# One issue table in place of a hand-written order: a chunked recurrence followed by a GELU block on one core

## The chip, the cores and the metric

The kernel runs on one core of one Trainium2 chip. The core has five engines that run in parallel, each through its own queue in program order: TensorE (PE) multiplies matrices and, as a separate instruction, loads their stationary operand (PEld); VectorE (DVE), ScalarE (ACT) and GpSimd (POOL) do elementwise work; SyncE (SP) issues transfers. Transfers are also issued here from the queues of ACT and POOL. The metric is the device time of one execution in microseconds (us); lower is better.

## The reference

Two blocks follow each other. The first is a recurrence over 768 time steps, for 4 batches and 8 heads, with a 40 x 40 state per head:

```python
for t in range(S):                                   # S = 768
    y[:, :, t] = einsum('bhd,bhde->bhe', r_t, state)
    Sa = einsum('bhde,bhe->bhd', state, a_t)
    state = state * w_t[:, :, None, :] - einsum('bhd,bhe->bhde', Sa, b_t)
    state = state + einsum('bhd,bhe->bhde', v_t, k_t)
```

The second takes the output as x with 3072 rows of 320 and computes `gelu(x @ w_in) @ w_out` with the exact GELU and an inner width of 2048. All inputs of the recurrence are 32-bit floats; the two weight matrices come as 64-bit floats, so the kernel reads 10.5 MB of weights (2 x 320 x 2048 x 8 bytes) and turns them into 32-bit floats itself.

## The kernel before

The 768 steps are cut into 12 chunks of 64 steps (`C = 64`, `NCH = 12`). Inside a chunk the recurrence is written as matrix products. For chunk c these are the steps, by the names of their functions and the tiles that the profile shows:

- `logs`, `sums`: ACT takes the logarithm of the decay w, PE sums it over time (`wT_ps`, `cum`), ACT takes exponentials (`wpT`, `en`, `part`).
- `turn_a`, `turn_b`, `turn_k`, `turn_v`, `turn_r`, `scale_a`, `scale_b`, `scale_k`: the inputs are transposed and scaled by the decay. For the first chunks PE does the transposes (`aT_ps`, `nT_ps`, ...), and ACT copies them out; for later chunks DVE does it with a stream transpose from tiles that are loaded in pairs.
- `make_N`, `make_A`, `make_RV`: products of 64 x 64 blocks, masked by DVE (`N`, `A`, `VR`).
- A triangular matrix has to be inverted for each chunk. N is written to device memory by SP (four transfers, L615), read back as 128 rows (`Nb`, two transfers, L664), and POOL runs 31 column steps of a multiply and an add each (`start_inverse`, L672 and L674) on `W`. The result goes back over memory (`store_inverse`, L686; `fetch_inverse`, L696 and L700), and `corner` and `joined` (`J`) complete it. Chunk 0 uses five rounds of PE products instead (`squares`, tile `sq`), each with an ACT copy, a DVE transpose and a DVE add between one round and the next.
- `make_av`, `make_X`, `make_sa`, `make_saT`, `make_M`, `make_y2`, `make_QY`: the chain through the state, ending in the two tiles `QY`.
- `outputs`: DVE makes `xt`, the new state `st`, and SP moves a few rows of `xt` between partitions with 11 transfers (L894, L897). `turn_state` transposes the state.

The MLP of a chunk (`mlp`) has four rounds of `ph` products with w_in (L993, 20 per half of the round's output, a GELU each on ACT), and then `po` products with w_out: 32 plain ones for the first three chunks (L1010), seven products of half blocks after that (`seven`, L946). It is a generator; `fill()` lets it issue its next piece between two recurrence steps.

The weights are converted by `to_float`: per piece, DVE and ACT steps (L319, L320, L321, L324), then either two more DVE steps (L327, L328) or two ACT steps and two POOL steps (L330 to L333). There are 10 pieces of w_in and 16 of w_out. w_in must be converted before the first `ph` of a column range, w_out before the first `po`.

The order is written out by hand, and no scheduler changes it: a long list of calls for chunks 0 to 2 with conversions between them (L1059 to L1242), then a loop over the chunks from 2 on (L1244), which issues loads two chunks ahead. Each call issues all instructions of its step, on all engines, at once. All PSUM tiles come from one pool of four equal buffers in rotation (`duo`, L96); a call of `keep(n)` lets the next `duo` run n x 128 columns of a product of no use first, so that PE stays occupied.

```python
    def duo(name):
        pt = psum.tile([P, 2, 512], FP32, tag="duo", name=name)
        while asked:
            n = asked.pop()
            mm(pt[:, 0, :n * P], ident, cum_m.unsqueeze(1).to_broadcast([P, n, P]))
        return pt
```

Of the kernel before, what the change touches and what calls it, by code (L numbers as in the profile page):

```python
# [19 lines left out]
def kernel(  # L20
# [12 lines left out]

# [23 lines left out]
    asked = []  # L90

    def keep(columns):

        asked[:] = [columns]

    def duo(name):  # L96
        pt = psum.tile([P, 2, 512], FP32, tag="duo", name=name)
        while asked:
            n = asked.pop()
            mm(pt[:, 0, :n * P], ident, cum_m.unsqueeze(1).to_broadcast([P, n, P]))  # L100
        return pt

# [8 lines left out]


    def ring(name, n, shape, zero, eng):
        tiles = []
        for i in range(n):
            t = const.tile(shape, FP32, name=f"{name}{i}")
            if zero is not None:
                eng.memset(zero(t), 0.0)
            tiles.append(t)
        turn = [0]  # L120

        def take():
            turn[0] += 1
            return tiles[(turn[0] - 1) % n]
        return take
# [4 lines left out]
    def whole(t):  # L130
        return t


    def unused(t, eng):
        for x in range(2):
            eng.memset(t[x * HP + BL:(x + 1) * HP, :, BW - BL:D + BL], 0.0)


    NT = 3

    NB = 4
    NS = 3
    paired = {n: const.tile([P, G * H, BW], FP32, name=n + "_pairs") for n in ("a", "v", "r")}
    w_tile = const.tile([P, G * DM + REST], FP32, name="w_tile")


    extra = const.tile([P, 4 * G * H * HP], FP32, name="extra")
    b_rows, k_rows = ([const.tile([P, G * DM + REST], FP32, name=f"{n}_rows{i}") for i in range(2)] for n in "bk")
# [3 lines left out]

    raws = {}

    def rows_of(src, c, e):

        return src[G * e:G * (e + 1), :, c * C:(c + 1) * C, :].rearrange("g h t d -> t (g h) d")

    def fetch(c, n, src, eng, t=None):
        if t is None:  # L160
            t = rows({"b": b_rows, "k": k_rows}[n][0 if c < NB else c % 2])
        for e in range(2):
            eng.dma_start(out=t[half(e)].rearrange("p g h d -> p (g h) d")[:, :, :D], in_=rows_of(src, c, e))
        raws[c, n] = t

    def fetch_pairs(c, n, src, eng, placed, t=None):


        if t is None:
            t = paired[n]  # L170
        rows = slice(c * C // 2, (c + 1) * C // 2)
        for x in range(2):
            for z, cols in enumerate((slice(0, D + BL), slice(BL, BW))):
                to = t[x * HP + z * BL:x * HP + (z + 1) * BL, :, :cols.stop - cols.start]
                if placed:
                    for e in range(2):
                        pairs = src[G * e + x].rearrange("h (s y) d -> s h (y d)", y=2)
                        eng.dma_start(out=to[:, e::2], in_=pairs[rows, :, cols])
                else:
                    pairs = src.rearrange("b (i x) (s y) d -> x s (b i) (y d)", x=2, y=2)[x]  # L180
                    eng.dma_start(out=to, in_=pairs[rows, :, cols])
        raws[c, n] = t

    def turn(to, c, n):

        nc.vector.transpose(to.rearrange("p n (s y) -> p n y s", y=2),  # L186
                            raws.pop((c, n)).rearrange("p n (y d) -> p n y d", y=2)[:, :, :, :BL])

    def load_w(c, t=None, eng=nc.sync):
        t = w_tile if t is None else t  # L190
        to = t[:, :G * DM].rearrange("p (g h d) -> p g h d", g=G, h=H)
        if c < NB:
            fetch(c, "w", w, eng, to)
        else:
            for e in range(2):
                for g in range(G):
                    eng.dma_start(out=to[half(e ^ g), g],
                                  in_=w[G * e + g, :, c * C:(c + 1) * C].rearrange("h t d -> t h d"))
        raws[c, "w"] = t

    def by_64(t):
        return t.rearrange("p n d -> p (n d)")[:, :G * H * HP].rearrange("p (n d) -> p n d", d=HP)

    def load_a(c, t=None, eng=nc.sync):
        if c < NT:
            fetch(c, "a", a, eng, by_64(paired["a"] if t is None else t).rearrange("p (g h) d -> p g h d", g=G))
        else:
            fetch_pairs(c, "a", a, eng, False, t)

    def load_kb(c):  # L210
        fetch(c, "b", b, nc.sync)
        fetch(c, "k", k, nc.sync)

    def load_VR(c):
        VR = turned_in.setdefault(c, {})["VR"] = VR_ring()
        for e in range(2):
            nc.sync.dma_start(out=VR[half(e)].rearrange("p g q m d -> p (g q m) d")[:, :, :D], in_=rows_of(v, c, e))

    def load_v(c):
        if c >= NT:  # L220
            fetch_pairs(c, "v", v, nc.sync, True)

    def load_r(c, eng=nc.sync):
        if c >= NT:
            fetch_pairs(c, "r", r, eng, True)
            return
        t = by_64(paired["v" if c == 1 else "r"]).rearrange("p (h g) d -> p h g d", g=G)
        for e in range(2):
            for g in range(G):
                eng.dma_start(out=t[half(e), :, g, :D],  # L230
                              in_=r[G * e + g, :, c * C:(c + 1) * C].rearrange("h t d -> t h d"))
        raws[c, "r"] = t

    ctx.enter_context(tc.manual_schedule(engines={mybir.EngineType.PE, mybir.EngineType.SP,
                                                 mybir.EngineType.DVE, mybir.EngineType.Pool,
                                                 mybir.EngineType.Activation}))

    st_ring = ring("st", 1, [P, 2, NP, G, HP], lambda t: t.rearrange("p e i g d -> p (e i g) d")[:, :, D:], nc.gpsimd)
    SM_ring = ring("SM", 1, [P, 2, G, NP, VC], None, None)
    early_b = work.tile([P, NK, TB], FP32, tag="xt", name="early_b").rearrange("p k t -> p (k t)")  # L240
    early_w = SM_ring().rearrange("p e g n c -> p (e g n c)")[:, :G * DM + REST]
    early_k = work.tile([P, G, NP, P], FP32, tag="rT", name="early_k", bufs=2).rearrange("p g n t -> p (g n t)")
    ahead = {n: t[:, :G * DM].rearrange("p (g h d) -> p g h d", g=G, h=H) for n, t in (("b", early_b), ("k", early_k))}
    spare_raw = work.tile([P, 4 * DM], UINT32, tag="spare", name="spare_raw")
    early_a = spare_raw.bitcast(FP32).rearrange("p (n d) -> p n d", d=BW)

    for t in w_tile, early_w:
        nc.gpsimd.memset(t[:, G * DM:], 0.0)
    load_w(0)
    fetch(0, "b", b, nc.sync)  # L250
    load_a(0)
    load_w(1, early_w)
    fetch(1, "b", b, nc.sync, ahead["b"])
    load_a(1, early_a)
    for t in (paired["a"], early_a):
        nc.gpsimd.memset(by_64(t)[:, :, D:], 0.0)

    one = const.tile([P, 1], FP32, name="one")
    nc.vector.memset(one, 1.0)
    nc.scalar.activation(one, one, ACT.Ln)  # L260


    ident = const.tile([P, P], FP32, name="ident")
    make_identity(nc, ident)


    cum_m = const.tile([P, P], FP32, name="cum_m")
    nc.gpsimd.memset(cum_m, 1.0)
    nc.gpsimd.affine_select(out=cum_m, in_=cum_m, compare_op=ALU.is_ge, fill=0.0, base=0,
                            pattern=[[1, P]], channel_multiplier=-1)  # L270
    nc.gpsimd.memset(cum_m[0:C, C:P], 0.0)

    upper = const.tile([P, C], FP32, name="upper")
    for e in range(2):
        nc.gpsimd.tensor_tensor(upper[half(e)], cum_m[half(e), half(e)], ident[half(e), half(e)], ALU.subtract)
    wp_ring = ring("wpT", 2, [P, G * NP * 2, C + 1], None, None)
    for _ in range(2):
        nc.gpsimd.memset(wp_ring()[:, :, 0], 1.0)
    padded = extra.rearrange("p (n g h d) -> p n g h d", n=4, g=G, h=H)
    nc.gpsimd.memset(pads(padded[:, 0]), 0.0)  # L280
    for n in range(1, 4):
        nc.gpsimd.memset(pads(padded[:, n]), 0.0)
    for t in b_rows + k_rows:
        nc.gpsimd.memset(t[:, G * DM:], 0.0)
    Tt_ring = ring("Tt", 1, [P, 2, G, NP, C], whole, nc.gpsimd)
    VR_ring = ring("VR", 2, [P, 2, G, NP, VC],
                   lambda t: t.rearrange("p g q m c -> p (g q m) c")[:, :, D:HP], nc.gpsimd)

    part_ring, avs_ring = (ring(n, 1, [P, 2, DM + REST], lambda t: t[:, :, DM:], nc.gpsimd) for n in ("part", "avs"))

    for n in "rv":
        nc.gpsimd.memset(by_64(paired[n])[:, :, D:], 0.0)

    def flat(t):
# [1073 lines left out]
```

## Time and profile before

| what | value |
|---|---|
| timed runs | 710.63 us (median), 710.3 and 711.71 |
| span of the profiled execution, first to last instruction | 709.1 us |
| what lies around it, median of the runs less span | 1.5 us |
| PE busy | 669.7 us, 94% |
| PEld busy | 587.1 us |
| DVE, ACT, POOL busy | 365.5, 222.3, 350.2 us |
| mean granted PE clock | 0.958 |
| bytes moved | 74.46 MB, 105 GB/s on average |

No separate clock of the profiled execution is given beside its span. The page cuts the span into 40 slices of 17.7 us. The granted clock is a share of full speed; the busy time of PE is modelled from pipelined instructions, so a busy PE need not be a fast one. A 32-bit product appears in the trace as two instructions. The first 20% of the span is where the weights are loaded and converted; the rest repeats with the chunks.

### The profile page before, as it was taken

The numbers are of one execution on the slowest core, as the hardware profiler recorded it, in microseconds if no ns is written. First come the engines' busy times: TensorE is split into PE (matmuls) and PEld (weight loads), VectorE is DVE, ScalarE is ACT, GpSimd is POOL, SyncE is SP. The second block draws the span as 40 slices with busy tenths as digits, with TensorE's granted clock in tenths as the row PEclk, the third lists the DMA queues.
The fourth block names the chain that finished last, engine by engine and source line by source line (L and its number), as shares of the span: only waits on it lengthen the run. The fifth ranks groups of instructions, "written<-read, shape, count | busy, mean of one in ns | idle before, by whom it ended". The sixth has DMA issues, their size and how long they took to land.

```text
span 709.1 us, 32732 instructions
## 1 busy us (share of the span) xinstructions
PE 669.7 (94%) x14778; PEld 587.1 (83%) x14778; DVE 365.5 (52%) x481; ACT 222.3 (31%) x308; POOL 350.2 (49%) x798
## 2 busy tenths in 40 slices
PE   7578897879999999999999999999999999999997
PEld 4567786757877877899899898998998898998987
DVE  2334689993354365375484483573671772522303
ACT  5124674444140240351241332232323413112020
POOL 5284458810851851861862853845836827800000
PEclk9775798999999999999999999999999999999999
DMA  9689538864667647656656747657648646020100
GB/s 130 121 167 151 104 87 203 136 128 88 123 122 113 132 94 110 133 100 113 124 102 121 137 87 128 125 93 128 133 84 144 130 86 85 20 55 4 31 8 19
DMA packets 287923, 74.46 MB, mean 105 GB/s; under 512 B 265736, under 2 KB 284456, under 8 KB 287784
## 3 DMA queue, kind: packets, MB, share of 16 engines
q1 hardware_dynamic: 283360, 68.20, 52.6%
q0 software_dynamic: 864, 2.36, 2.2%
q8 instruction: 116, 1.90, 1.2%
q10 hardware_dynamic: 3560, 1.80, 1.0%
q14 instruction: 23, 0.19, 0.1%
HBM read 58.69 MB, written 9.70 MB: 96 GB/s over the span
## 4 chain that ended last, share of the span: by engine, by line
PE 81%; DVE 6%; DMA 3%; ACT 3%; SPq 3%; issue 2%; ACTq 1%; DVEq 0%
PE ph L993 26%; PE po L946 19%; PE po L1010 7%; PE QY L110 6%; PE J L110 2%; PE av L110 2%; PE A_ps L110 2%; PE X L110 2%; PE sq L110 2%; PE RV_ps L110 2%; DMA a_pairs<-in_a_dram 2%; PE sap L110 2%; PE saT_ps L110 2%; PE M_ps L110 2%; PE wT_ps L110 1%
## 5 line engine op out<-in xcount | busy, mean ns | idle before, releaser
L993 PE MATMUL ph<-xt,w_in_sb 64*128 64x256 f32 x1920 | 219.4, 381 | 0.0
L672 POOL TENSOR_TENSOR tmp<-W,Nb 128x126 f32<-128x126 f32 (+22 forms) x310 | 124.3, 401 | 160.0 <-DMA Nb<-N 137.0
L993 PEld LDWEIGHTS ph<-xt,w_in_sb 64*128 64x128 f32 x1920 | 182.4, 187 | 22.1 <-issue 0.3
L674 POOL TENSOR_TENSOR W<-W,tmp 128x126 f32<-128x126 f32 (+22 forms) x310 | 132.4, 427 | 24.3
L995 ACT ACTIVATE gt<-ph 128x1024 f32<-128x1024 f32 x48 | 49.1, 1024 | 152.5 <-PE ph L993 152.3
L946 PE MATMUL po<-w_out_sb,gt 128*128 128x160 f32 x576 | 83.0, 302 | 0.1
L946 PEld LDWEIGHTS po<-w_out_sb,gt 128*128 128x128 f32 x576 | 78.7, 190 | 2.2 <-DVE gt L966 0.4
L1010 PE MATMUL po<-w_out_sb,gt 128*128 128x320 f32 x192 | 55.8, 448 | 1.1 <-ACT wpT L443 1.1
L1010 PEld LDWEIGHTS po<-w_out_sb,gt 128*128 128x128 f32 x192 | 36.7, 195 | 16.7 <-issue 1.5
L186 DVE STREAM_TRANSPOSE aT<-a_pairs 128x1024 f32<-128x1024 f32 x9 | 11.2, 1247 | 46.6 <-DMA a_pairs<-in_a_dram 46.6
L802 DVE COPY Tt<-J 32x512 f32<-32x512 f32 x9 | 6.2, 689 | 54.5 <-ACT Tt L802 54.5
L786 ACT COPY Js<-J 128x256 f32<-128x256 f32 x11 | 4.1, 370 | 94.6 <-PE J L110 94.6
L998 DVE TENSOR_TENSOR half<-gt 128x1024 f32<-128x1024 f32 x9 | 11.4, 1271 | 29.6 <-ACT gt L995 29.6
L946 PE MATMUL po<-extra,half 128*128 128x160 f32 x176 | 26.1, 303 | 0.0
L320 ACT ACTIVATE conv<-conv,rebias 128x320 uint32<-128x320 uint32 (+1 forms) x26 | 16.1, 624 | 29.0 <-DVE conv L319 23.1
L575 DVE TENSOR_TENSOR SM<-M_ps,upper 128x1024 f32<-128x1024 f32 x12 | 14.5, 1207 | 19.7 <-PE M_ps L110 19.7
L946 PEld LDWEIGHTS po<-extra,half 128*128 128x128 f32 x176 | 24.2, 190 | 0.3
L995 ACT ACT_TABLE_LOAD x10 | 12.8, 1283 | 36.0 <-PE ph L993 36.0
L950 DVE TENSOR_TENSOR os<-os,po 128x160 f32<-128x160 f32 x36 | 11.5, 319 | 23.6 <-PE po L946 17.9
L946 PE MATMUL po<-extra,gt 128*128 128x160 f32 x144 | 21.0, 299 | 0.0
L662 POOL MEMSET W<- 128x512 f32 x10 | 5.3, 528 | 31.5 <-DMA inv<-W 31.5
L886 DVE TENSOR_TENSOR xt<-QY,wpT 128x512 f32<-128x512 f32 x24 | 15.4, 684 | 10.2 <-PE QY L110 9.6
(224 smaller groups left out, 1134.7 us busy)
## 6 DMA issues: line engine op xcount, KB each, us to landing
Nb<-N SPq DMA_DIRECT2D x20, 256.0 KB
VR<-in_v_dram SPq DMA_DIRECT2D x24, 160.0 KB
out_dram<-os SPq DMA_DIRECT2D x48, 80.0 KB
b_rows<-in_b_dram SPq DMA_DIRECT2D x22, 160.0 KB
k_rows<-in_k_dram SPq DMA_DIRECT2D x22, 160.0 KB
N<-N SPq DMA_DIRECT2D x44, 64.0 KB
Tt<-inv SPq DMA_DIRECT2D x44, 64.0 KB
a_pairs<-in_a_dram SPq DMA_DIRECT2D x18, 144.0 KB
```

The costliest lines, as they stand in the source:

```text
L110: nc.tensor.matmul(o, lhsT, rhs, start=first, stop=True, skip_group_check=True)
L320: nc.scalar.activation(power, power, ACT.Relu, bias=rebias, scale=8.0)
L575: nc.vector.tensor_tensor(to, pt, upper.unsqueeze(1).to_broadcast([P, 2 * G * NP, C]), ALU.mult)
L672: eng.tensor_tensor(t, W[:, :rows, j:j + 1].to_broadcast([P, rows, rest]), Nb[:, j:j + 1, j + 1:].to_broadcast([P, rows, rest]), ALU.mult)
L674: eng.tensor_tensor(W[:, :rows, j + 1:], W[:, :rows, j + 1:], t, ALU.add)
L886: nc.vector.tensor_tensor(xt[:, :NP, g * P:(g + 1) * P].rearrange("p i (e t) -> p i e t", e=2), Y, wp[:, g, :, :, :C], ALU.mult)
L946: nc.tensor.matmul(po[:, n, :DM // 2], l_[:, f], r_[:, f], start=f == 0, stop=f == NF // 2 - 1)
L950: nc.vector.tensor_tensor(to, one_, other, ALU.add)
L993: nc.tensor.matmul(ph[:, x, s], w_in_sb[half(x), kt, p * P:(p + 1) * P], xt[half(x), kt], start=kt == 0, stop=kt == NK - 1)
L995: nc.scalar.activation(gt[:, 4 * q:4 * q + 4].rearrange("p (x s) t -> p x s t", x=2), ph, ACT.Gelu)
L998: nc.vector.tensor_tensor(s1, block(1, 0), block(1, 1), ALU.add)
L1010: nc.tensor.matmul(po[:, g], gt[:, f, g * P:(g + 1) * P], w_out_sb[:, f], start=f == 0, stop=f == NF - 1)
```

## The change

The functions compute the same things, but each is now a generator that stops after every part: one product, one copy, one transfer. A table names the parts in the order in which they are issued, over all chunks and the start. An entry is `name.chunk`, then optionally `@engine` (which engine does a copy or issues a transfer), `#banks` (which of four PSUM buffers its tiles take), `+n` (n x 128 columns of the useless product first) and `*n` (n parts in a row).

```diff
+    def on(default):
+        return asked["on"] or default
+    def copy(to, given, default):
+        eng = on(default)
+        (eng.copy if eng is nc.scalar else eng.tensor_copy)(to, given)
     def duo(name):
-        pt = psum.tile([P, 2, 512], FP32, tag="duo", name=name)
-        while asked:
-            n = asked.pop()
+        banks = asked["banks"]
+        if banks:
+            pt = psum.tile([P, 2, 512], FP32, tag=f"duo{banks.pop(0)}", name=name, bufs=1)
+        else:
+            pt = psum.tile([P, 2, 512], FP32, tag="duo", name=name)
+        n, asked["columns"] = asked["columns"], 0
+        while n:
+            some, n = min(n, 4), n - min(n, 4)
...
     def make_N(c):
-        masked(flat(N), products("N_ps", t["nT"], t["aT"], True))
+        pt = products("N_ps", t["nT"], t["aT"], True)
+        yield
...
+        masked(flat(N), pt)
+        yield
...
+                dma(blk[j, z].rearrange("n s t -> s n t"), flat(N)[at:at + BL, :, z * BL:(z + 1) * BL])
+                yield
...
+    def go(name, c, on_=None, columns=0, banks=""):
+        if (name, c) not in begun:
+            begun[name, c] = steps[name](c)
+        asked.update(on=engines.get(on_), columns=columns, banks=list(banks))
+        return next(begun[name, c], "end") != "end"
...
+        load_w.0*2 logs.0 zeros.3 zeros.10 zeros_a.0 zeros_w.0 masks.0 zeros.2 zeros.14 zeros.13 zeros.5 zeros.4
+        masks.0 sums.0#0+4 sums_rows.0#1+2 sums_rows.0 load_a.0 zeros.1 load_b.0*2 scale_b.0 sums.0 load_a.0
+        turn_a.0#2+4 load_w.1 turn_b.0#3 turn_b.0 load_a.1 scale_a.0 make_N.0#1+4 load_w.1 logs.1 sums.1#0+4
+        load_in.0 load_in.2 warm.0 sums_rows.1#2 load_a.1 masks.0 make_N.0 zeros.0 squares.0 load_b.1 squares.0
...
+        load_v.8*2 load_bt.9*2 second.6*4 load_bt.9 load_r.9*2 make_A.8#0 load_k.8 make_A.8 second.6 new_state.7
```

(`load_in` and `first_float` load and convert w_in, `load_out` and `second_float` w_out; `first` and `second` are the two halves of `mlp`.) Set side by side, the two instruction lists differ in this:

- PE: the same products, 7,491 against 7,520 matrix instructions. The useless products grow from 6 with 1,536 columns to 35 with 9,728 columns; 27 of these, 8,704 columns, lie ahead of the first `ph`. The runs of large products (`ph`, `po`) between small ones become 90 instead of 76.
- Order on PE: the first `ph` comes before `sap` of chunk 1 instead of after it, and in one run of 50 products; the first `po` comes after 80 `ph` products, as before. From chunk 3 on the order of the recurrence steps stays nearly the same, with single `ph` or `po` pieces set between other pairs of them.
- DVE and ACT: some copies change engine (12 halves of `saT`, 4 of `Js`, 2 of `turned` and others go to DVE; 4 of `SM` go to ACT): DVE 483 to 507 instructions, ACT 326 to 294.
- SP: 748 to 758 transfers; the 10 w_out transfers that ACT issued are SP's. The first w_in transfer is SP's tenth issue instead of its 29th, and w_in transfers stand between those of the inputs; the last w_out transfer is its 174th issue instead of its 166th.
- POOL: the same 800 instructions. The two POOL steps of one w_in piece come ahead of the column steps of chunk 1's inverse instead of after; the other six pieces stay behind them.

## The prediction

> **What bounds the kernel now.** I read the page first: busy time per engine and the row of the granted clock. PE is busy for 94% of the span, so at first sight there is little to win; but the clock row shows a start at less than full speed.
>
> ```profile
> PE 669.7 (94%) x14778; PEld 587.1 (83%) x14778; DVE 365.5 (52%) x481; ACT 222.3 (31%) x308; POOL 350.2 (49%) x798
> ...
> PEclk9775798999999999999999999999999999999999
> ```
>
> Then the table of busy times by stretches, cut where the PE's order in time shows landmarks: 99.3 is the first `ph`, 164.7 the `ph` after `joined` of chunk 2, 225.7 `corner` of chunk 3, 656 the last `QY`. The columns are PE, PEld, DVE, ACT, POOL, then granted clock, DMA share and GB/s.
>
> ```profile
> 0.00:50.00 50.00, 34.23 (x992) 27.34 (x996) 14.57 (x17) 17.68 (x20) 26.28 (x74) 0.86 0.86 142
> 50.00:80.00 30.00, 25.29 (x721) 23.04 (x721) 14.68 (x22) 13.24 (x20) 16.28 (x34) 0.50 0.84 148
> 80.00:99.30 19.30, 18.38 (x594) 15.03 (x590) 14.43 (x20) 13.67 (x20) 6.14 (x6) 1.00 0.27 67
> 99.30:164.70 65.40, 54.06 (x1096) 44.92 (x1093) 58.87 (x102) 30.47 (x43) 39.38 (x78) 0.90 0.68 141
> 164.70:225.70 61.00, 59.96 (x994) 47.24 (x986) 25.34 (x34) 17.90 (x23) 25.88 (x67) 1.00 0.57 111
> 225.70:656.00 430.30, 429.17 (x10025) 383.63 (x10024) 224.46 (x267) 123.73 (x173) 236.26 (x541) 1.00 0.57 104
> ```
>
> From 164.7 to 656 PE lacks 2.2 us of 491.3 and has the full clock. In the timeline a 64-row product of a kind takes the same time in every chunk there (`RV_ps` 0.98, `saT_ps` 1.13, 20 `ph` 4.52). Nothing can be won there by a new order, only lost. Up to 164.7 PE is idle for 15.8 + 4.7 + 0.9 + 11.3 = 32.7 us, and 25.3 us of its work between 50 and 80 run at half clock. There the bound changes by stage. Lines of PE and POOL in order of time (start, duration, tile, in brackets the idle time before and what ended it):
>
> ```profile
> 35.93 0.24 POOL L672 TENSOR_TENSOR st<-st,spare_x 128x31 f32<-128x31 f32 x1 [8.05 <-DMA spare_x<-N]
> ...
> 63.35 0.23 POOL L674 TENSOR_TENSOR st<-st 128x16 f32<-128x16 f32 x1
> ```
>
> ```profile
> 82.59 0.74 PE L110 MATMUL J<-L,N 32*32 32x32 f32 x64 [0.15 <-PE vT_ps L110]
> ...
> 94.11 1.02 PE L110 MATMUL RV_ps<-cum_m,ident 128*128 128x512 f32 x2
> ...
> 99.34 4.59 PE L993 MATMUL ph<-xt,w_in_sb 64*128 64x256 f32 x40
> ```
>
> The inverse of chunk 1 occupies POOL from 35.9 to 63.6, and `corner` of chunk 1 comes at 82.6 because PE is late with chunk 0, not because of the inverse. Last, the transfers as SP issues them (the timeline of its queue):
>
> ```profile
> 26.09 2.97 SPq L615 DMA_DIRECT2D N<-N  x4
> 30.65 1.13 SPq L664 DMA_DIRECT2D spare_x<-N  x2
> 31.82 3.15 SPq L383 DMA_DIRECT2D w_out_sb<-in_moe_w_in_dram  x4
> ```
>
> An issue costs SP 0.5 to 1.2 us. Added up, 167 issues take 133.4 us of the first 164.7, and 468 take 338.6 of the 374.3 us between 225.7 and 600: SP is at 90% all along.
>
> **Part 1, up to the first `ph` (99.3 before).** The products ahead of it, at their full-clock prices, are some 49 us: three times `wT_ps` 0.93, `cum` 1.3, `aT_ps`, `nT_ps` 0.9, `N_ps` 1.0 (15); five rounds of `sq` (8.7); two each of `kT_ps`, `A_ps`, `vT_ps`, `rT_ps`, `av`, `RV_ps` near 1 (12); `saT_ps`, `sap`, `M_ps` and both `QY` (6); `J` four times, `X`, `tn_ps` (5); the three of `warm` (1.4). The useless products add 8,704 columns. One of 512 takes 1.02 us in the row of 94.11, so 17 us where 1,536 columns cost 3. Together 66 us, so PE alone is not the bound: I go by the chain that frees `ph`.
> Up to `N` of chunk 1 nothing gets shorter (w, b, a are issued first in both): mask at 24.8 before, 26 after, since w_in transfers now stand among its inputs. SP stores `N` as issues 30 to 33 and reads it back as 36 and 37. At 0.85 us each that is 31 us, as before. POOL then starts at 36 to 37 and needs 27.7 us, say 29 with DVE busier: 65.5. From the last column step to the landing of the fetched result the trace shows 9 us (63.6 to 72.6, the next release on POOL); two or three w_in and b transfers among them make 11 and more, so `corner` of chunk 1 is at 79. Behind it, in the new PE order, come `X`, `cum`, `vT_ps`, `J`, `tn_ps`, `nT_ps`, `RV_ps`, `N_ps` with copies between: 10 us. First `ph` at 89. Of w_in, the last pieces for it are issued just behind the stored inverse (issue 80, 70 to 72), land by 76 and take 7 us of conversion: 83, hidden.
> Does chunk 0 keep pace? `sq` round 4 ended at 51; between rounds the chain is copy 0.58, transpose 0.72, add 0.65, some 2.2 us, and the old order puts `kT_ps`, `A_ps`, `vT_ps`, `rT_ps` into one gap. In the new one they lie elsewhere, so it ends near 45. The 29 us from there to `QY` hold 14 us of full-clock products plus seven evacuations near 1 us: 22, so 67. `av`, `rT_ps`, `wT_ps`, `aT_ps` end at 71. It has 8 us of room before 79. `sap` of chunk 1 (1.0) is no longer ahead, so 99.3 compares to 98: gain 9. Bounds: nothing if `corner` is as late as before, and 21.4 us, all the idle time of this part. I take 9, the chain.
>
> The clock decides how much of that room is real. The trace has 0.50 for all of 50 to 80, with PE busy 84% of the time and no idle gap above 1.4 us. It has 1.00 at 84 to 100, where four useless products stand among the same small ones. [...]
>
> **Part 2, from there to `corner` of chunk 3 (225.7).** Before, the part to 164.7 loses 11.3 us of idle and about 5.4 of clock (54.1 x 0.10): 17. The largest:
>
> ```profile
> 115.90 3.05 PE L110 MATMUL QY<-SM,extra 64*64 64x104 f32 x64 [4.27 <-DVE SM L575]
> ...
> 152.94 0.74 PE L110 MATMUL J<-L,N 32*32 32x32 f32 x64 [2.88 <-DVE L L772]
> ```
>
> Both are DVE queues: 58.9 of 65.4 us busy with conversions. After, DVE has 37 us of work behind it at `corner` of chunk 1 and 65 more to the last w_out piece by the prices of uncontended rows (0.32, 0.32, 0.48, 0.49, 0.49 per piece; with POOL beside it their means are 0.47, 0.46, 0.65, 0.70, 0.53, so up to 75): 79 + 75 = 154, where it was 168.9. PE's own products up to the same `po` (89 plus 50 `ph` 11.3, then 55 us of the rest) come to 156, so the two are level, with little cover. SP's last w_out transfer is issue 174: at 0.81 us, 141; the 10 issues that ACT gave up cost 7 us of it and are covered. I leave 7 us of waits for the 17: gain 10. Bounds: 17, and a loss of 7 if POOL and DVE collide as they do before at 115 to 135.
>
> **Part 3, what the saturated part pays.** There 20 `ph` between others take 4.52; 80 in one run take 17.46, 4.37 per 20. So each break costs 0.15, and the small product beside it 0.06 (1.54 for `QY` before `po`, 1.48 before `QY`). 14 more runs x 0.21 = 2.9. Useless products behind the first `ph`: 1,024 columns, 1.9. Copies have shorter covers: `J` to `J2` 3.3 us instead of 4.5, `J2` to `sap` 2.3 instead of 4.5, `A` to `av` 3.2 as it was; the copies need 0.4 to 1.2. I put 1.2 us on them in all. Bounds: 0, and 1.2 us at each of two places in nine chunks, 21.6. At the end `xt` needs 1.4 on DVE, 5.0 of issues on ACT, about 2 to land, and PE has 40 `po`, 11.3 us, over it (15.9 before): covered. Copies moved to DVE (about 8 us over the whole run, DVE 52% busy) and two more table loads on ACT (1.28 each, ACT 31% busy) lie beside PE. SP's 10 more issues likewise. Loss 6.
>
> **Sum.** 709.1 - 9 - 10 + 6 = 696.1; the median of the runs is 1.5 above the span: 697.6, given as 697.
>
> **Rivals.**
> - The clock is not held. Then chunk 0's chain keeps the half clock (14 us more for its products), the useless products double to 34 us, the room of 8 us is gone, and part 1 gains 2 and part 2 6: 710.6 - 8 + 6 = 708, or 705 if part 2 keeps its gain. For it: `sq` rounds at 24 to 36 throttled although PE worked. Against it: the stage from 84 on.
> - SP's queue is the bound (slower). A chunk needs 65 issues; by the rows 46 us of the 50.7 that a chunk takes. Single transfers now wait in line behind others whose tile is not yet free. From 4.7 us of such waits per chunk on, SP sets the period; it eats the gain of 13 at 6.1 us per chunk (9 chunks x 1.4), and at 7 the result is 710.6 - 13 + 21 = 718. For it: loads of 2 chunks ahead in between `xt` and `Tt` transfers. Against it: SP now issues even earlier than the PE needs, and the trace shows no such stall on PE.
> - Everything in the start works: idle time and clock of parts 1 and 2 all regained (21 + 17, less 6, less the 10 that DVE's sum forbids): 688, and down to 684.
>
> **How the numbers follow.** Main case 0.50; clock 0.20; SP 0.20; all regained 0.10. Main range 690 to 704. Leaving out the far half of the last and half of the SP case gives 685 to 716. A difference of 0.2%, 1.4 us, is about what these runs can tell from none. Faster: 0.50 + 0.10 + 0.16 of the clock case = 0.76; same 0.04; slower 0.20.
>
> **What would show it.** First `ph` near 89; POOL's inverse of chunk 1 again at 36 to 65; granted clock over 0.8 between 50 and 80; idle PE before `corner` of chunk 3 under 25 us, that `corner` near 207; from there to the last `QY` the same 429 us to within 5. If that stretch is longer, part 3 or SP's queue was wrong; if `ph` is later than 95, the chain of part 1.

## The result, and the profile after

The changed kernel takes 740.51 us (median of four runs, 737.69 to 742.1) against 711.17 before: 1.040 times as long, 95% interval 1.037 to 1.043. The forecast was 697. Ratios compare means and leave out executions that took over 1.5% more than the fastest of their kernel. The profiled execution took 737.69, its span is 735.9, 26.8 longer than before.

The page after, cut to the lines shown before, and the first line of its chain of work that ended last, with the same line of the kernel before under it:

```profile
PE 690.3 (94%) x14836; PEld 600.3 (82%) x14836; DVE 379.2 (52%) x505; ACT 215.0 (29%) x286; POOL 375.3 (51%) x798
...
PEclk9997799999999998998999999998999989999999
...
PE 47%; POOL 23%; DMA 11%; SPq 9%; issue 6%; DVE 3%; ACT 1%; DVEq 0%; POOLq 0%; ACTq 0%
```

```profile
PE 81%; DVE 6%; DMA 3%; ACT 3%; SPq 3%; issue 2%; ACTq 1%; DVEq 0%
```

PE's share, 94%, is what it was. Two things are new: the clock has dents all along the span, and the chain that sets the end runs over POOL, transfers and SP's queue for 43% of the span; in the kernel before, PE alone had 81% of it and POOL did not appear.

Busy time by stretches of the changed kernel, cut at the same landmarks: 102.2 is the first `ph`, 216.9 `corner` of chunk 3, 686 lies in the last `QY` (it ends at 687.7); the columns are PE, PEld, DVE, ACT, POOL, clock, DMA share, GB/s.

```profile
0.00:50.00 50.00, 40.47 (x916) 27.23 (x916) 20.44 (x26) 18.38 (x23) 20.27 (x55) 0.97 0.90 137
50.00:80.00 30.00, 26.29 (x763) 22.53 (x765) 14.16 (x20) 9.94 (x14) 24.96 (x57) 0.74 0.89 153
...
102.20:168.00 65.80, 64.70 (x1276) 54.63 (x1278) 56.42 (x107) 33.96 (x46) 33.52 (x72) 0.97 0.70 143
168.00:216.90 48.90, 47.87 (x884) 37.13 (x886) 17.43 (x21) 11.13 (x16) 26.79 (x68) 1.00 0.49 96
216.90:686.00 469.10, 446.69 (x9995) 399.38 (x9997) 240.18 (x287) 122.33 (x161) 259.92 (x540) 0.97 0.53 98
```

`corner` of chunk 3 comes at 216.9 instead of 225.7: the start gained 8.8 us. From there to `corner` of chunk 9 it is 335.6 us instead of 304.3, 31.3 lost, and from there to the end 183.5 instead of 179.1, 4.4 lost. 31.3 + 4.4 - 8.8 is the 26.9 of the two spans. Two rows cut at these corners, the first of before, the second of after:

```profile
225.70:530.00 304.30, 303.58 (x7057) 270.25 (x7056) 170.02 (x199) 92.39 (x129) 175.87 (x408) 1.00 0.63 115
```

```profile
216.90:552.50 335.60, 320.83 (x7107) 284.31 (x7109) 178.23 (x210) 91.68 (x121) 196.81 (x407) 0.96 0.57 104
```

PE is idle for 14.8 us instead of 0.7; that is 14 of the 31. A clock of 0.96 instead of 1.00 over 335.6 us costs 13 more by estimate (335.6 x 0.04). The other 4 are large products that the new order has in this stretch instead of behind it (60 more instructions of `ph`, 16 fewer of `po`), so they are not a loss.

**Where PE waits, and for whom.** Between 217 and 600, PE's longest wait in total is that of `J` (`corner`) for L, the fetched inverse (sum, times, longest):

```profile
PE J L103 <- DVE L L814: 10.4, 4, 3.2
```

One chunk of the changed kernel in order of time (start, duration, engine, tile, in brackets the idle time before):

```profile
488.03 1.22 DVE L610 TENSOR_TENSOR N<-N_ps,upper 128x1024 f32<-128x1024 f32 x1
489.25 0.23 POOL L706 TENSOR_TENSOR W<-W,tmp 128x16 f32<-128x16 f32 x1
489.78 1.63 POOL L74 DMA_DIRECT2D inv<-W  x2 [0.30 <-POOL W L706]
494.01 0.84 SPq L74 DMA_DIRECT2D Tt<-inv  x2
496.49 0.71 DVE L814 STREAM_TRANSPOSE L<-Tt 128x512 f32<-128x512 f32 x1 [5.54 <-DMA Tt<-inv]
497.34 0.74 PE L103 MATMUL J<-L,N 32*32 32x32 f32 x64 [1.87 <-DVE L L814]
499.01 2.64 SPq L74 DMA_DIRECT2D N<-N  x4
503.21 1.13 SPq L74 DMA_DIRECT2D Nb<-N  x2
508.28 0.24 POOL L704 TENSOR_TENSOR tmp<-W,Nb 128x31 f32<-128x31 f32 x1 [13.34 <-DMA Nb<-N]
```

Read it as a ring: each step waits for the one before it, and the last step releases the first one of the next chunk. POOL ends the inverse of one chunk at 489.5; SP waits for the stored result and fetches it from 494.0 on. N of the next chunk is ready at 489.2, but its store stands behind the fetch in SP's queue and goes at 499.0; `Nb` follows at 503.2, and POOL, idle for 13.3 us, starts again at 508.3, works for 34.2 us, and the ring closes. From one stored N to the next it is 55.6 us (219.7 to 553.0, six chunks). In the kernel before, PE needed 50.7 for a chunk. What SP waits for between 217 and 600, after and then before (sum, times, longest):

```profile
SPq L74 <- DMA inv<-W: 62.0, 7, 11.0
```

```profile
SPq L615 <- DVE N L575: 8.2, 3, 3.7
SPq L696 <- DMA inv<-W: 3.4, 3, 2.1
```

62.0 us in seven chunks is 8.9 per chunk; before, SP waited 3.4 us for the inverse, and 8.2 for N's mask, as it should where PE sets the pace. And the same ring stood in the kernel before, in lines that the forecast did not read: N of chunk 5 stored and `J` of chunk 4, then N of chunk 10 and `J` of chunk 9.

```profile
271.36 1.94 SPq L615 DMA_DIRECT2D N<-N  x4
278.58 0.75 PE L110 MATMUL J<-L,N 32*32 32x32 f32 x64
...
528.25 2.03 SPq L615 DMA_DIRECT2D N<-N  x4
530.01 0.75 PE L110 MATMUL J<-L,N 32*32 32x32 f32 x64
```

N's store runs 7.2 us ahead of `J` at first and 1.8 at the end: it took 51.6 us from one stored N to the next (218.5 to 528.2, six chunks), 0.9 more than PE, and lived on a reserve that lasted just to the last chunk. The first two of these turns, 52.9 and 52.5, were set by N's mask: N left as soon as it was masked. From chunk 7 on it left 0.3, 1.4, 1.9 and 3.4 us behind its mask, as the fetch stood ahead of it, in turns of 51.2, 51.2 and 51.6. In the changed kernel N of chunk 4 is stored at 219.7, no earlier than before (218.5), while PE is 8.8 us further. The reserve is spent at once, and from then on each chunk costs what the ring costs.

The ring also grew, from 51.6 to 55.6. Most of that is POOL: its 62 steps of an inverse took 31.6 us before and 34.9 after (means of chunks 4 to 9). With the copies back on their old engines (experiment 4) they take 34.8, with the ring open (experiment 1) 31.5. Why they grew was not tested by itself: whether the order of DVE's work made them longer, or the waiting in the ring put more of that work beside them, stays open.

### The profile page after: what moved, and what is told of

It is laid out like the page before. It is cut to its first block, busy times and chain, and to the rows that moved or that the text cites. A ratio compares the mean times of both kernels' runs of the same rounds, so it can differ in the third digit from the quotient of the medians.

```text
span 735.9 us, 32773 instructions
## 1 busy us (share of the span) xinstructions
PE 690.3 (94%) x14836; PEld 600.3 (82%) x14836; DVE 379.2 (52%) x505; ACT 215.0 (29%) x286; POOL 375.3 (51%) x798
## 3 DMA queue, kind: packets, MB, share of 16 engines
q1 hardware_dynamic: 286720, 69.84, 51.6%
## 4 chain that ended last, share of the span: by engine, by line
PE 47%; POOL 23%; DMA 11%; SPq 9%; issue 6%; DVE 3%; ACT 1%; DVEq 0%; POOLq 0%; ACTq 0%
PE ph L1005 17%; POOL W L706 11%; POOL tmp L704 10%; SPq L74 9%; PE po L1050 7%; PE po L1029 4%; PE QY L103 4%; DMA Nb<-N 3%; DMA inv<-W 3%; DMA N<-N 1%; PE J L103 1%; PE sap L103 1%; PE saT_ps L103 1%; PE M_ps L103 1%; PE wT_ps L103 1%
## 5 line engine op out<-in xcount | busy, mean ns | idle before, releaser
L1005 PE MATMUL ph<-xt,w_in_sb 64*128 64x256 f32 x1920 | 229.9, 392 | 7.9 <-ACT part L477 5.7
L704 POOL TENSOR_TENSOR tmp<-W,Nb 128x126 f32<-128x126 f32 (+22 forms) x310 | 139.2, 449 | 177.1 <-DMA Nb<-N 153.9
L1005 PEld LDWEIGHTS ph<-xt,w_in_sb 64*128 64x128 f32 x1920 | 189.0, 193 | 33.2 <-ACT part L477 5.8
L706 POOL TENSOR_TENSOR W<-W,tmp 128x126 f32<-128x126 f32 (+22 forms) x310 | 141.5, 456 | 24.3
L1029 PE MATMUL po<-w_out_sb,gt 128*128 128x320 f32 x192 | 54.0, 437 | 0.0
L71 ACT COPY os<-po 128x160 f32<-128x160 f32 (+1 forms) x22 | 6.3, 312 | 65.0 <-PE po L1050 41.2
L1050 PE MATMUL po<-extra,gt 128*128 128x160 f32 x144 | 24.7, 331 | 0.0
L71 ACT COPY Tt<-J 32x512 f32<-32x512 f32 x15 | 8.6, 576 | 54.3 <-DVE Tt L71 37.9
L1050 PEld LDWEIGHTS po<-extra,gt 128*128 128x128 f32 x144 | 22.8, 213 | 0.5
L814 DVE STREAM_TRANSPOSE L<-Tt 128x512 f32<-128x512 f32 x11 | 7.8, 709 | 29.2 <-DMA Tt<-inv 29.2
```

The source lines that it names most:

```text
L71: (eng.copy if eng is nc.scalar else eng.tensor_copy)(to, given)
L704: nc.gpsimd.tensor_tensor(t, W[:, :rows_, j:j + 1].to_broadcast([P, rows_, rest]), Nb[:, j:j + 1, j + 1:].to_broadcast([P, rows_, rest]), ...
L706: nc.gpsimd.tensor_tensor(W[:, :rows_, j + 1:], W[:, :rows_, j + 1:], t, ALU.add)
L1005: nc.tensor.matmul(ph[:, x, s], w_in_sb[half(x), kt, p * P:(p + 1) * P], xt[half(x), kt], start=kt == 0, stop=kt == NK - 1)
L1029: nc.tensor.matmul(po[:, g], gt[:, f, g * P:(g + 1) * P], w_out_sb[:, f], start=f == 0, stop=f == NF - 1)
L1050: nc.tensor.matmul(to, l_[:, f], r_[:, f], start=f == 0, stop=f == NF // 2 - 1)
```

## The experiments

The runs came in five groups, each on one chip; the kernel before had medians of 710.4, 714.5, 713.0, 713.2 and 711.7 in them, so ratios are compared across groups. The changed kernel itself was 1.040 in one group and 1.034 in another, so a difference of half a per cent between groups says little. Every kernel computes the whole reference.

**1. The stores of N ahead of the fetch,** and the loads of `Nb` behind its first two transfers. Table entries moved, for N of chunks 4 to 10 (here chunk 8; `...` marks entries left out):

```
-  fetch_inverse.7*2 inverse.8 make_X.7#2 load_v.7*2 fetch_inverse.7 load_r.8 make_N.8 make_X.7 ... make_N.8*2 turn_v.7 make_N.8*2
+  inverse.8 make_X.7#2 load_v.7*2 load_r.8 make_N.8*5 fetch_inverse.7*2 inverse.8*2 fetch_inverse.7 make_X.7 ... turn_v.7
```

> The changed kernel with one thing moved: for chunks 4 to 10 SP issues the four stores of N ahead of the fetch of the inverse of the chunk before, and the two loads of Nb behind the first two transfers of that fetch. All other engines keep their order. Theory Q (queue): N of the next chunk, masked at 489.2, is stored only at 499.0 because it stands behind the fetch in SP's queue, and the fetch waits for POOL; that closes a loop POOL - fetch - store of N - Nb - POOL of 55.6 us per chunk. With N stored when it is masked the loop falls below PE's 50.7, so seven chunks get about 4.8 us shorter: 740.5 - 34 = 706, with PE's waits for L gone from chunk 4 on. Theory B (breaks): PE itself is slower by its many short runs and switches, and the loop only follows it: 738 to 742. Theory D (collision): POOL's column steps take 35 us instead of 32 because DVE does more beside them; moving the stores leaves that: 732 to 740.

Measured: 724.1 (1.017; interval 1.013 to 1.022), about half of what was expected; on a later group 729.7 (1.023). The waits of SP and the order on the queue, after the edit:

```profile
SPq L74 <- DVE N L610: 33.9, 7, 9.1
```

```profile
431.25 1.94 SPq L74 DMA_DIRECT2D N<-N  x4
433.31 2.45 SPq L74 DMA_DIRECT2D Tt<-inv  x2
...
438.38 0.74 PE L103 MATMUL J<-L,N 32*32 32x32 f32 x64 [0.86 <-DVE L L814]
```

The ring is open: the waits for the stored inverse fall from 62.0 to 0.5 us, and the fetch goes 11 to 23 us after POOL's last step, where 4.5 are needed. But the fetch now stands behind N, which waits for its mask, so L is late for `J` six times by 0.2 to 2.4 us:

```profile
PE J L103 <- DVE L L814: 9.0, 6, 2.4
```

From `corner` of chunk 3 to that of chunk 9 it is 325.0 us instead of 335.6. PE's idle time in it falls only from 14.8 to 11.6; the larger part of the gain is the clock, 0.99 instead of 0.96. The 16 us gained show that the ring is a cause; part of the rest is the same fault with the sides exchanged.

**2. The same stores from ACT's queue.** `make_N.x*2` became `make_N.x*2@a` for chunks 4 to 11.

> The changed kernel with the four stores of N of chunks 4 to 11 issued from ACT's queue, at the same places of the table; the loads of Nb stay behind the fetch in SP's queue. Theory Q: N leaves 5 to 9 us earlier, but Nb still stands behind the fetch, so only the time from the fetch to the stored N (5 us and the landing) comes out of the loop: period 55.6 to 51 or 52, total 710 to 720. Theory B: 740. Theory D: 735 to 740.

Measured: 727.6, from 718.7 to 738.4 (1.019; 1.012 to 1.026). N leaves at 314.0 where the fetch is at 318.6, so N no longer waits, but `Nb` still stands behind the fetch and other loads (325.4). Less than expected, with a wide spread; whether ACT's copies, which now stand behind N's stores, are the reason is not shown.

**3. The ring in the kernel before, lengthened.**

```
...
             run(steps)
+            for _ in range(20):
+                nc.gpsimd.memset(inverse_tmp[n2], 0.0)
             store_inverse(n2, (nc.gpsimd,))
```

> The kernel before, with 20 fills of tmp (about 0.2 us each, 4 us) added on POOL between the last column step and the store of the inverse, for chunks 4 to 11. Theory Q: the same loop stands in the kernel before at 51.4 us per chunk, 0.7 above PE's 50.7, and had a reserve of 7 us at chunk 4 that was down to 1.8 at chunk 10; 4 us more per chunk come through nearly whole: 8 x 4.0 less 2 = 30 more, 741. If POOL has room, as its 49% busy share says: 711 to 713.

Measured: 743.8 (1.046; 1.043 to 1.049), 33 us more. The 20 fills take 5.5 us in the trace, not 4, so 44 in the eight chunks:

```profile
425.29 5.51 POOL L1333 MEMSET tmp<- 128x146 f32 x20
```

The first three chunks behind `corner` of chunk 3 still take 52.8, 50.3 and 50.3 us, as before (52.9, 50.4, 50.2): the reserve pays for them. The next five take 54.5 to 56.4, which is the ring's 51.2 and the fills less 1. So POOL, busy for half of the span, had that reserve and no more room. SP's waits for the stored inverse are of the kind that the changed kernel has:

```profile
SPq L698 <- DMA inv<-W: 44.2, 7, 9.9
```

**4. Copies back on their default engines** (every `@a` and `@v` of chunks 3 to 11 removed).

> The changed kernel with every copy of chunks 3 to 11 on the engine that it had by default (all engine marks removed), table order unchanged. Theory D: the copies given to DVE are what lengthens POOL's column steps from 32 to 35 us; back on ACT, eight chunks get 3 us shorter: 716. Theory Q: the steps are longer because they now lie beside other DVE work (24 us of DVE inside them instead of 16.4), of which these copies are some 2 us per chunk, worth half of that on POOL: 732 to 738. Theory B: 740.

Measured: 738.6 (1.039; 1.036 to 1.043). They are not the cause.

**5. Two transfers of the fetch, then N, then `Nb`, then the rest** (`fetch_inverse.7*2 make_N.8*5 inverse.8*2 fetch_inverse.7 ...`).

> The changed kernel with SP's order in chunks 4 to 10: the first two transfers of the fetch, then the four stores of N, then the two loads of Nb, then the other four of the fetch. Theory Q: from the end of POOL's steps to the start of the next ones it was 18.8 us in the changed kernel (489.5 to 508.3); with N 4 us and Nb 4 us earlier about 14, and with 35 us of steps a loop of 49, just below PE's 50.7; the fetch no longer stands behind N as in the run with the stores first (724.1, where L still came 1 to 2.4 us late six times), so 712 to 722. If what is left of the loss in that run is not SP's order but PE's own pace or DVE beside POOL: 724 or more.

Measured: 734.2 (1.026; 1.021 to 1.031): no better than the first experiment. The ring is open there as well, but `J` then waited 10.0 us in five chunks for `Tt` itself, up to 4.1, since other loads that waited stood ahead of the fetch.

**6. The open ring, lengthened by the same fills** (5.5 us here too).

> The run with the stores first (724.1) with the same 20 fills of tmp (4 us) on POOL between the last column step and the store of the inverse, chunks 4 to 11. Theory Q: there the stores of N opened the loop; POOL ends 5 to 20 us before N of the next chunk is masked (524.4 to 536.9, 475.4 to 483.3), so the 4 us are hidden: 722 to 728. If POOL's loop still bounds that run: 724 + 30 = 754.

Measured: 737.8 (727.8 to 740.6; 1.027). The total, between the two expectations, does not settle it, as the start of the profiled execution took longer: `corner` of chunk 3 at 224.7, where equal instructions gave 217.5 and 220.2 in others. From that corner to the one of chunk 9 it is 328.8 us; in the first experiment it was 325.0. Six times 5.5 would be 33, so nearly all of the fills is hidden there, as the theory of the queue has it.

**7 and 8. The start, on top of experiment 1:** all useless products taken out; then only those ahead of N of chunk 1, with `warm` behind it.

> The run with the stores first without any useless products (all 35 removed). Theory H (they hold the clock): granted clock between 50 and 80 back to 0.5, the products of chunk 0 slower by 5 to 10 us, total 728 to 733. Theory N (they only cost): N of chunk 1, masked at 34.4 instead of 24.8 before, comes 4 us earlier, and so does all behind it: 718 to 721. Both together near 724.

> The run with the stores first, and only the part up to N of chunk 1 changed: no useless products ahead of it, and the products of warm behind it instead of ahead. All later ones stay. If the start is set by N of chunk 1 and POOL's steps behind it: N masked near 28 instead of 36, POOL's steps from 39 instead of 46, first ph at 95 instead of 102, total 724 less 5 to 7 = 717 to 719. If the start is set by the conversions or by chunk 0: first ph within 2 us of 102, total 722 to 725.

Measured: 739.4 (1.033) and 734.3 (1.028), against 1.017 and 1.023 for experiment 1; neither lies where it was expected. In the first, the clock between 50 and 80 is 0.61, and `corner` of chunk 3 comes at 228.6. In the second, N of chunk 1 was stored at 32.0 instead of 36.0 and POOL began at 44.0 instead of 46.3, yet the first `ph` came at 105.9 (102.3 and 105.8 in experiments 5 and 6, of the same group): an earlier N of chunk 1 bought nothing, with these useless products gone.

**9 to 12. Other ways to open the ring,** in one group: experiment 1 again; with the two next parts of large products moved ahead of `corner`; the changed kernel with only the fetch on POOL's queue (`fetch_inverse.x@g`, chunks 3 to 10); all three together.

> The same kernel as the first experiment (stores of N ahead of the fetch), run again beside the next three, because the start of equal programs came 5 to 7 us apart between the two groups of runs. Theory Q: 1.017 times the kernel before, as before, 723 to 728.

> The run with the stores first, and in chunks 3 to 9 the two next parts of the large products (some 2.3 to 4.5 us of PE) moved from behind corner (L on DVE, J on PE) to ahead of it. In that run L came 0.2 to 2.4 us late for J, since the fetch now stands behind N on SP; and DVE, waiting for L, held back a sum of po, which cost 3.4 us of PE and 4 us at 0.59 clock at 330. Theory Q: these waits go, 10 to 14 us less: 710 to 715 where the run above has 724. If the rest of the loss is in PE's own pace: within 2 us of it.

> The changed kernel (740.5), table order untouched, with the fetch of the inverse of chunks 3 to 10 issued from POOL's queue instead of SP's; POOL has nothing to do then but wait for Nb. Theory Q: neither N nor anything else stands behind the fetch on SP (62 us of such waits between 217 and 600 in the changed kernel, 3.4 before), N goes when it is masked; POOL pays 5 us of issues per chunk, a loop of 33 + 11 = 44: PE bounds again, 700 to 712. If the waits only change their place (POOL's issues, Nb): 725 to 740.

> The three together: stores of N first, corner two parts later, fetch on POOL's queue. Theory Q: nothing is left of the loop and of the waits for L; from corner of chunk 3 (217) on 50.7 us per chunk as before, total 710.6 - 8 = 702, at most 708. If PE's own pace is part of the loss: 715 or more.

Measured: 729.7 (1.023), 734.5 (1.032), 731.1 (1.025), 724.4 (1.018). The second failed: `J`'s wait for L fell to 6.1 us, but T came 2.7 late and `Tt` 1.4. In the third the wait only changed its place: N was stored at 430.4, then SP stood for 8.3 us before a load of `v_pairs` whose tile DVE had not read yet, and `Nb` behind it went at 442.8. The fourth has no wait for L left and still misses its 702. Its longest wait is this (DVE, PE and SP in order of time):

```profile
335.19 0.58 SPq L74 DMA_DIRECT2D r_pairs<-in_r_dram  x1
339.66 1.25 DVE L504 STREAM_TRANSPOSE rT<-r_pairs 128x1024 f32<-128x1024 f32 x1 [5.60 <-DMA r_pairs<-in_r_dram]
340.83 0.28 DVE L1046 TENSOR_TENSOR os<-os,po 128x160 f32<-128x160 f32 x1
341.17 9.03 PE L1005 MATMUL ph<-xt,w_in_sb 64*128 64x256 f32 x54 [4.17 <-DVE os L1046]
```

A load of r stands behind `Nb` (334.0) on SP; the transpose of it, not needed before the next chunk, stands on DVE ahead of a sum of `po`; the sum frees the bank that `ph` was given by the table; PE waits 4.2 us and then runs slowly (54 `ph` in 9.0 instead of 6.1).

**13 to 15. That entry moved; the changed kernel again; and without useless products,** in one group.

```
-  corner.5#1 fetch_inverse.5@g turn_v.5 load_v.6 turn_r.6 load_VR.6 second.3 make_X.5 ... make_RV.5#3 load_a.7*2
+  corner.5#1 fetch_inverse.5@g turn_v.5 load_v.6 load_VR.6 second.3 make_X.5 ... make_RV.5#3 turn_r.6 load_a.7*2
```

> The run with all three changes of the steady part (stores of N first, corner two parts later, fetch on POOL's queue), and one table entry moved: turn_r of chunk 6 behind make_RV of chunk 5, eleven entries later. In that run PE lacked 4.2 us at 341, behind a sum of po on DVE that stood behind this transpose, which waited 5.6 us for a late load of r; the clock fell to half for some 4 us after it. Theory W (in-order queues pass a late transfer on): this chunk, 61.4 us there, becomes 53 to 54 and the total 6 to 9 us less than without it, 715 to 719. If the chunk is long only because it holds more of PE's work: less than 2 us.

> The changed kernel once more, on the same chip as the other two of this group, so that they have a reference: 1.040 times the kernel before, 739 to 744.

> The changed kernel without its 35 runs of useless products. Theory H (they hold the clock in the start): corner of chunk 1 at 95 to 97 instead of 87.7, corner of chunk 3 6 to 9 us later than with them; since POOL's loop, not PE, sets the pace behind it, N of chunk 4 and the total move by the same: 746 to 750. Theory N (they only cost PE time): corner of chunk 1 at 84 or earlier, total 735 to 738.

Measured: 715.5 (ten runs from 706.7 to 720.5; 1.001, 0.997 to 1.004), 738.9 (1.034; 1.030 to 1.038) and 747.6 (1.043; 1.035 to 1.050). One part of the table's 2,064, moved, goes with a loss that is 12 us smaller in ratio (the two kernels ran in different groups), and the chunk in question goes from 61.4 us (first row, experiment 12) to 54.1 (second row, this one):

```profile
333.90:395.30 61.40, 57.23 (x1226) 51.47 (x1224) 29.97 (x41) 16.62 (x21) 30.99 (x74) 0.94 0.55 103
```

```profile
327.20:381.30 54.10, 54.10 (x1230) 49.54 (x1229) 32.08 (x41) 16.70 (x21) 34.99 (x74) 1.00 0.59 116
```

7.3 of the 12 us are in this chunk; where the rest lies is not shown. So four moves, in SP's, POOL's and DVE's order and of some large products on PE, take the change from 3.4% slower to equal with the kernel before, and not beyond. Two of the stretches between the same corners, experiment 1 and this one, show what is left of the waits:

```profile
217.50:542.60 325.10, 313.47 (x7107) 277.83 (x7110) 173.20 (x210) 91.86 (x121) 176.86 (x407) 0.99 0.59 108
```

```profile
224.30:533.40 309.10, 306.17 (x7067) 271.90 (x7068) 177.72 (x210) 91.59 (x121) 205.18 (x439) 0.99 0.56 111
```

PE is idle for 2.9 us here, and the stretch is 4.8 us longer than before. The useless products hold the clock of the start: the stretch from 50 to 80 without them and with them:

```profile
50.00:80.00 30.00, 19.65 (x672) 17.34 (x663) 12.42 (x17) 9.56 (x14) 21.79 (x51) 0.68 0.85 143
```

```profile
50.00:80.00 30.00, 23.95 (x769) 20.01 (x772) 14.79 (x20) 10.96 (x16) 25.67 (x59) 0.90 0.91 153
```

`corner` of chunk 1 is at 92.9 without and 87.0 with them, `corner` of chunk 3 at 222.4 and 216.9.

**16 and 17. Two more spots:** the fill of W for chunk 10 behind `scale_k` of chunk 9; and chunk 3 back in the changed kernel's order.

> The run that equalled the kernel before (e13: stores of N first, corner two parts later, fetch on POOL's queue, turn_r of chunk 6 later), with one POOL entry more moved: the fill of W for chunk 10 behind scale_k of chunk 9. There a ph at 578 came 2.15 us late and 7.14 us long for 48 products instead of 5.4, behind the exponential part on ACT, which waited 6.7 us for scale_k on POOL, which stood behind the fill of W, which waited for the stored inverse. Theory W (in-order queues pass a late transfer on): 3 to 4 us less, 0.995 to 0.996 times the kernel before. If such spots don't add up: 1.000.

> As e16, but the stores of N ahead and the later corner only from chunk 4 on, chunk 3 in the changed kernel's order: in e13 the 40 ph at 213.6 came 1.35 us late behind the mask of N and took 6.28 instead of 4.6. Theory W: 2 to 3 us less than e16, 0.991 to 0.993. If chunk 3's corner then waits for L as it did in the first experiment (2.4 us): same as e16 or 2 us more.

Measured: 715.8 (twelve runs from 708.0 to 721.0; 1.003, 1.000 to 1.006) and 723.1 (1.016; 1.013 to 1.020). In the first, PE's wait at 578 fell from 2.15 to 0.35 us and the total didn't follow. In the second, chunk 4's `corner` waited 6.05 us for L, the ring's price for one chunk. No version was found that beats the kernel before. What stays open is where the gain of the start, 8.8 us, is now lost, and why runs of this kernel spread over 13 us; no single wait over 2.2 us is left between 217 and 600 in experiment 13. One part can be estimated: PE is busy for 677.7 us in that trace, at a clock of 0.98, where it was 669.7 at 0.96; the 8,192 more columns of useless products, at 1.02 us for 512, are 16 us of its work.

## Why the prediction was wrong, point by point

- **"Nothing can be won there by a new order, only lost"**: right. **"Part 3 ... Loss 6"** is the step that failed. Its terms were priced by PE's own rows: breaks 2.9, useless products 1.9, covers of copies 1.2. Measured are 31.3 to `corner` of chunk 9 and 4.4 behind it. Where nothing waits its terms look fair: with the ring opened and one late transpose moved (experiment 13), the chunks from `corner` of chunk 6 to that of chunk 9 take 50.4, 51.0 and 50.7 us with the same small parts and breaks, where before they took 50.1, 50.6 and 50.1: 0.4 per chunk, 4 in nine. (The three chunks ahead of them still had waits: 53.5, 49.4 and 54.1, before 52.9, 50.4 and 50.2.) The missing term is the ring over SP and POOL: 4 us per chunk longer than before, with no reserve.
- **The rival "SP's queue is the bound"** was the mechanism. It had 0.20 and 718. Its threshold of 4.7 us of waits per chunk was passed (8.9; its own sum would then have given 46 + 8.9 = 54.9 per chunk, close to the 55.6), but its place was not named: not any load in line behind another, but N's store behind the fetch. And "the trace shows no such stall on PE" was the wrong test. What mattered was a reserve, 7.2 us falling to 1.8, which the lines of SP and PE of the kernel before show. Read from there, the sum would have been: the ring's 51.6 per chunk stands whatever the start gains, so nothing of parts 1 and 2 can reach the end. That the ring itself would grow by 4 us could not be read from it. (SP "at 90% all along" is 133.4 of 164.7, 81%, in the start.)
- **Part 1, first `ph` at 89**: it came at 102.2 (98 before, in that order). The step "mask at 24.8 before, 26 after" failed: N of chunk 1 was masked at 34.4. The first product waited 4.9 us for POOL, useless ones and `warm` stood ahead of `nT`, and POOL's steps ran from 46.0 to 75.3 instead of 36 to 65.5. The useless products are the smaller part of this: with none of them (experiment 7) the mask comes at 33.2, with those ahead of it gone and `warm` behind it (experiment 8) at 30.8. There `nT` still stands behind a round of `sq`, and b of chunk 1 is issued at 11.8 instead of 7.8, so "w, b, a are issued first in both" did not hold. The length forecast for POOL's steps, 29, was right. From `corner` of chunk 1 to the first `ph` it is 14.5 us where 10 were put. With N earlier (experiment 8) the first `ph` was as late, so N was not the only thing that held it; what else did is not shown.
- **The clock under the useless products**: granted clock 0.74 between 50 and 80 (0.90 in another run), 0.50 before, 0.68 without the useless products. They are worth 8.8 us in the total (experiments 14 and 15). The direction was right; "over 0.8" was not reached in the first profile, and in neither of these two the full clock that part 1 counted on for the products of chunk 0. What in them decides was not tested: they add work and also fill gaps (PE is busy for 24.0 of these 30 us with them, experiment 14, and for 19.7 without, experiment 15).
- **Part 2, gain 10**: measured 114.7 us from the first `ph` to `corner` of chunk 3 instead of 126.4, 11.7, one of them `sap`, which no longer counts here. Right.
- **The end**, covered by forecast: behind the last `QY` it is 48.2 us instead of 53.0. The 4.4 lost behind `corner` of chunk 9 lie ahead of it, 135.2 us instead of 126.1; a `ph` there waited 5.7 us for an exponential on ACT.
- **DVE at 52%, copies beside PE**: costed at nothing, and nothing came back when they were undone (experiment 4). But DVE's work inside POOL's steps grew from 16.4 to 24 us per inverse, and POOL's steps from 32.0 to 35.2 (medians; below), which is most of what the ring grew. That was in no term.

## What to carry to other kernels

A saturated engine is not the only bound: follow one chunk round every ring that crosses queues (store, load, compute, store, load), take its period, and look at how its reserve changes from chunk to chunk; a second ring close to the first (here 51.6 us beside PE's 50.7) can show as soon as the first gets ahead, as it did here by 8.8 us. When an order is rewritten, look in each in-order queue for the transfer that waits longest, and for what stands behind it that is ready; a late entry that nobody needs yet can stop PE through three queues (for 4.2 us in experiment 12). Small reorderings that free one queue can only move the wait (8.3 us on SP in experiment 11), so each has to be read again in the trace.

## What the runs showed of the hardware

- From chunk 3 on, POOL's 62 steps of an inverse last longer the more DVE works beside them: over the 36 inverses of chunks 3 to 11 in four kernels (before, after, experiments 1 and 13) the length is 23.5 us + 0.48 us per us of DVE busy time inside it (correlation 0.96; 27.5 us with 9.7 of DVE, 36.6 with 27.4). The inverse of chunk 2 does not follow this: with 30 us of DVE beside it, conversions for the most part, it takes 32.0 to 32.4 us in all four. So it is not DVE's busy time alone that counts; which of its instructions lengthen POOL's steps was not separated here.
- PE's clock fell to 0.50 after idle gaps of 2.40 and 1.35 us, and stayed at 1.00 after others of 2.35 and 1.53. In experiment 1, PE was idle for 2.40 us before 217.5, and these are the 2 us stretches around it (clock third from the end):

```profile
215.00:217.00 2.00, 0.13 (x1) 0.00 (x0) 0.33 (x1) 0.00 (x0) 0.00 (x0) 1.00 0.65 98
217.00:219.00 2.00, 1.48 (x68) 1.35 (x70) 1.26 (x4) 0.00 (x0) 0.00 (x0) 0.70 0.93 242
219.00:221.00 2.00, 2.00 (x12) 1.65 (x10) 1.78 (x2) 0.00 (x0) 0.49 (x2) 0.50 1.06 129
```

  A gap of 1.53 us in the same run (542.6) left it at 1.00, and so did one of 2.35 ahead of the next `J` (271.1 to 273.4; first two rows below). In experiment 13 a gap of 1.35 us (212.3 to 213.6) brought it down (last two rows):

```profile
273.00:275.00 2.00, 1.57 (x71) 1.43 (x72) 2.00 (x4) 0.37 (x1) 0.00 (x0) 1.00 0.95 241
275.00:277.00 2.00, 2.00 (x22) 1.80 (x20) 1.21 (x2) 0.00 (x0) 0.49 (x2) 1.00 1.35 155
...
213.00:215.00 2.00, 1.41 (x8) 1.19 (x10) 1.16 (x2) 0.00 (x0) 1.01 (x2) 0.77 0.29 47
215.00:217.00 2.00, 2.00 (x12) 1.66 (x10) 0.00 (x0) 0.00 (x0) 0.00 (x0) 0.50 0.75 123
```

  Behind the gap of 2.40 us, 1.6 us were lost in 4 (2 x 0.30 + 2 x 0.50). The length of one gap does not decide it in these four cases; what does was not shown.
- From which queue a transfer is issued changed the total (1.019 and 1.025 in experiments 2 and 11, against 1.040 and 1.034 in two groups of the changed kernel), the data moved being the same: on SP a transfer whose data are ready waits behind one whose data are not (N, masked at 489.2 in the changed kernel, was stored at 499.0). SP's waits for the stored inverse, which N and others stood behind, were 62.0 us in seven chunks there; in experiment 11, with the fetch on POOL's queue, SP's largest wait in total was 38.9 us, for N's mask.
